# Threshold attention with a dense block: q and k loaded as 32-token by 32-dim quadrant blocks and transposed by VectorE in SBUF instead of by TensorE through PSUM

## Chip, cores and metric

One core of one Trainium2 chip. The metric is the device time of one execution in microseconds (us). Three or four executions of each kernel were timed, and the median is quoted. On a single core no second core can tell a slow execution from a fast one, so an execution more than 1.5% above the fastest of its kernel is called slow and left out of comparisons.

## The reference

Attention over 8 batches of 8 heads, 576 tokens, head dimension 64. In each row only the scores within tau of the row's maximum are kept. A dense block of width 2,048 follows, with h·relu6(h+3)/6 as its activation.

```python
scale  = 1.0 / np.sqrt(64)
scores = scale * np.matmul(q, k.transpose(0, 1, 3, 2))          # 8 x 8 x 576 x 576
thresh = np.max(scores, axis=-1, keepdims=True) - tau           # tau = 0.02
scores = np.where(scores >= thresh, scores, -1e9)
attn   = softmax(scores)                                        # (sum + 1e-9)
x      = np.matmul(attn, v) -> 4608 tokens x 512
h      = x @ w_in                                               # 512 -> 2048
out    = (h * np.clip(h + 3.0, 0.0, 6.0) / 6.0) @ w_out         # 2048 -> 512
```

## The kernel before

The work is cut into 16 "quads" of four heads, each quad into two pairs of heads, and each quad into nine "slots". A slot makes 128 rows of scores for two heads, and in slot 8 the last 64 tokens of all four. In every slot TensorE makes the scores of the next slot, and hidden and output products of an earlier batch. VectorE copies the scores out of PSUM (where this kernel's TensorE results go) into SBUF (where its loads go) and takes their maxima; GpSimd makes the small bias (tau less the maximum); ScalarE masks and takes exponentials; GpSimd normalises into `pn`; and one DMA transpose on SyncE's queue turns `pn` into `pT`, one slot later. TensorE multiplies `pT` by v ("the attention product") in slot 6 for the first pair and in slot 1 of the next quad for the second.

q and k come in natural layout, in pieces (runs of bytes that lie together) of 256 bytes, and have to be transposed to have the head dimension on the partitions:

```python
def main(i, h):                                   # i: q or k
    src = (q, k)[i]
    nc.sync.dma_start(out=nat[quad][i][0][:, :, h, :],
                      in_=src[b, 4 * g + h, 0:512, :].rearrange("(p t) d -> p t d", t=4))
...
def transpose_main(pair, i):
    main = nat[pair // 2][i][0]
    ps = ps_m.tile([P, 512], F32, tag="m", name="tp")
    for t in range(4):
        nc.tensor.transpose(ps[:, t * P:(t + 1) * P], main[:, t, 2 * (pair % 2):2 * (pair % 2) + 2, :], identf[:])
    def evict():
        if i == 0:
            nc.scalar.activation(out=qkT[pair][0][:, 0:512], in_=ps[:], func=Act.Copy, scale=scale)
        else:
            nc.scalar.copy(out=qkT[pair][1][:, 64:576], in_=ps[:])
    return evict
```

The loop over slots, cut to the order in which things are issued:

```python
for n, sl in enumerate(queue):
    if slot == 4 and quad + 2 < NQUAD:
        load_quad(quad + 2)                       # only lists the loads; they start below
    ...                                           # exponentials of the slot before
    sm_max(sl)
    if slot != 6 and todo1:
        ...                                       # hidden product, relu, gate
    ...                                           # output product, masks
    if slot == 1 and quad > 0:   av_main(2 * quad - 1)
    elif slot == 2 and quad > 0: av_rest(quad - 1)
    elif slot == 6:              av_main(2 * quad)
    elif slot > 2 and quad + 1 < NQUAD:
        ...                                       # TensorE transposes q or k (slots 3, 4, 5, 7, 8)
    queue[n + 1].tiles = scores(queue[n + 1].quad, queue[n + 1].slot)
    if prev is not None:
        sm_norm(prev)                             # pn of the slot before, and its DMA transpose
    flush()                                       # stores
    start(loads, 2 if n < 3 else 1)               # one step of two q or k loads, on SyncE's queue
    start(vcasts or casts, 1 if n else 0)         # v and weight loads, on GpSimd's queue
```

The transpose of slot 3, which completes the first pair, is issued at the end of slot 4, and slot 6's attention product needs it.

Of the kernel before, what the change touches and what calls it, by code (L numbers as in the profile page):

```python
# [21 lines left out]
def kernel(  # L22
# [49 lines left out]
    casts = []  # L72
    vcasts = []

    def load_quad(quad):
        b, g = divmod(quad, 2)
        nat[quad] = []
        for nm in "qk":
            nat[quad].append((nat_pool.tile([P, 4, 4, D], F32, tag=nm + "m", name=nm + "m"),
                              nat_pool.tile([64, 4, D], F32, tag=nm + "r", name=nm + "r")))  # L80

        def main(i, h):
            src = (q, k)[i]
            nc.sync.dma_start(out=nat[quad][i][0][:, :, h, :],
                              in_=src[b, 4 * g + h, 0:512, :].rearrange("(p t) d -> p t d", t=4))

        def rest(i):
            src = (q, k)[i]
            nc.sync.dma_start(out=nat[quad][i][1][:],
                              in_=src[b, 4 * g:4 * g + 4, 512:S, :].rearrange("h p d -> p h d"))  # L90

        for n in range(2):
            for i in range(2):
                loads.append(lambda n=n, i=i: [main(i, 2 * n + a) for a in range(2)])
        loads.append(lambda: [rest(i) for i in range(2)])

    def load_v(b):
        vm = v_pool.tile([P, H, 4 * D], BF16, tag="vm", name="vm")
        vr = v_pool.tile([P, NPAIR, D], BF16, tag="vr", name="vr")
        vsb[b] = (vm, vr)  # L100
        for g in range(2):
            vcasts.append(lambda g=g: nc.gpsimd.dma_start(
                out=vm[:, g * 4:g * 4 + 4, :],
                in_=v[b, g * 4:g * 4 + 4, 0:512, :].rearrange("h (p t) d -> p h (t d)", t=4)))
        for a in range(2):
            vcasts.append(lambda a=a: nc.gpsimd.dma_start(
                out=vr[a * 64:(a + 1) * 64, :, :],
                in_=v[b, :, 512:S, :].rearrange("(hp a) p d -> a p hp d", a=2)[a]))
# [4 lines left out]
    def load_weights():  # L113
        for n4 in range(4):
            for ki in range(KI):
                casts.append(lambda n4=n4, ki=ki: nc.gpsimd.dma_start(
                    out=w_in_sb[:, ki, n4 * 512:(n4 + 1) * 512],
                    in_=moe_w_in[ki * P:(ki + 1) * P, n4 * 512:(n4 + 1) * 512]))
        for ni in range(NI):
            casts.append(lambda ni=ni: nc.gpsimd.dma_start(  # L120
                out=w_out_sb[:, ni, :], in_=moe_w_out[ni * P:(ni + 1) * P, :]))
# [5 lines left out]
    load_quad(0)  # L127
    start(loads, 5)
# [3 lines left out]
    identf = singles.tile([P, P], F32)  # L132
    make_identity(nc, identf)
# [9 lines left out]
    def alloc_qk(pair):  # L143
        qkT[pair] = (qk_pool.tile([P, S], F32, tag="qT", name="qT"),
                     qk_pool.tile([P, S + 64], F32, tag="kT", name="kT"))

    def transpose_main(pair, i):
        main = nat[pair // 2][i][0]
        ps = ps_m.tile([P, 512], F32, tag="m", name="tp")
        for t in range(4):  # L150
            nc.tensor.transpose(ps[:, t * P:(t + 1) * P], main[:, t, 2 * (pair % 2):2 * (pair % 2) + 2, :], identf[:])  # L151

        def evict():
            if i == 0:
                nc.scalar.activation(out=qkT[pair][0][:, 0:512], in_=ps[:], func=Act.Copy, scale=scale)
            else:
                nc.scalar.copy(out=qkT[pair][1][:, 64:576], in_=ps[:])
        return evict

    def transpose_rest(pairs):  # L160
        ps = ps_m.tile([P, 512], F32, tag="m", name="tr")
        for n, pair in enumerate(pairs):
            for i in range(2):
                nc.tensor.transpose(ps[:, (2 * n + i) * 64:(2 * n + i + 1) * 64],
                                    nat[pair // 2][i][1][:, 2 * n:2 * n + 2, :], identf[:64, :64])

        def evict():
            for n, pair in enumerate(pairs):
                qT, kT = qkT[pair]
                src = ps[:, 2 * n * 64:(2 * n + 1) * 64], ps[:, (2 * n + 1) * 64:(2 * n + 2) * 64]  # L170
                nc.scalar.activation(out=qT[:, 512:S], in_=src[0], func=Act.Copy, scale=scale)
                nc.scalar.copy(out=kT[0:64, S:S + 64], in_=src[1][0:64, :])
                nc.scalar.copy(out=kT[64:P, 0:64], in_=src[1][64:P, :])
        return evict

    def keys(pair, a, hf):
        kT = qkT[pair][1]
        c0 = 64 * (1 - a) + hf * HALF
        return kT[a * 64:(a + 1) * 64, c0:c0 + HALF]
# [35 lines left out]
    def sm_mask(sl, i):  # L215
        s = sl.s[:, i, :]
        nc.scalar.activation(out=s, in_=s, func=Act.Prelu, bias=sl.bias[:, i:i + 1], alpha=REJECT)  # L217
# [114 lines left out]
    for i in range(2):  # L332
        transpose_main(0, i)()
# [155 lines left out]
```

## Time and profile before

| | before |
|---|---|
| time, median of 3 | 635.71 us (633.47 to 638.48) |
| span of the profiled run, mean granted TensorE clock (share of the full clock) | 631.7 us, 0.965 |
| first slot-8 scores at | 41.6 us |
| quads 1 to 4 (slot 8 to slot 8), while weights come in | 148.3 us |
| quads 5 to 13, mean | 34.34 us |
| quads 14 and 15, for which no q or k is loaded | 33.0, 33.8 us |
| tail after the last quad | 66.1 us |

The five stages are cut at the scores of slot 8, from the trace's records. They add up to the span, so that a difference of two kernels can be put into its stages. The timeline view gives start, length, queue, line, operation and count of what SyncE issues in two slots of one quad, in the kernel before:

```profile
352.78 1.30 SPq L236 DMA_TRANSPOSE pT<-pn  x1
354.17 1.27 SPq L84 DMA_DIRECT2D qm<-in_q_dram  x2
...
356.33 1.29 SPq L236 DMA_TRANSPOSE pT<-pn  x1
```

A transpose takes SyncE 1.3 us to issue and a pair of loads another 1.3. With 3.55 us per slot there is room, and each transpose is issued on time.

### The profile page before, as it was taken

To read this page: it belongs to the slowest core of one execution; us is meant where nothing else is said; L and a number is where in the kernel's file an instruction comes from. 1 tells how busy PE (TensorE), PEld (TensorE's weight loads), DVE (VectorE), ACT (ScalarE), POOL (GpSimd) and SP (SyncE) were. 2 spreads that over 40 slices of the span, in tenths; PEclk is the share of its full clock that TensorE was granted. 3 is DMA by queue.
4 is the path that set the end of the run, shared out by engine and by line. 5 is a ranking of instruction groups with operands and counts; after the bars stand their busy time and mean duration, and the time that the engine had idled before them with its cause. 6 is when DMAs were issued, how large, how long until landed. Compare 5 with 4: busy or idle time off the path is not lost.

```text
span 631.7 us, 11524 instructions
## 1 busy us (share of the span) xinstructions
PE 560.2 (89%) x3840; PEld 323.5 (51%) x3840; DVE 423.8 (67%) x1024; ACT 472.2 (75%) x1062; POOL 305.6 (48%) x646
## 2 busy tenths in 40 slices
PE   4976677876898999899998999899998999898997
PEld 2543334444555555455555555455555555454563
DVE  0453447665787888678887888788886887783260
ACT  2795879647887898779897989788885989773250
POOL 0575568654555654555455544564555545452000
PEclk9987788978999999999999999999998999999999
DMA  4599999999568884787589667788497857453102
GB/s 108 80 188 142 154 147 154 165 137 153 101 102 158 130 175 99 164 119 156 110 158 154 143 137 129 132 141 166 106 170 104 163 116 110 83 102 89 67 4 81
DMA packets 269498, 80.45 MB, mean 127 GB/s; under 512 B 252544, under 2 KB 264832, under 8 KB 269440
## 3 DMA queue, kind: packets, MB, share of 16 engines
q1 hardware_dynamic: 252032, 70.81, 59.1%
q0 software_dynamic: 17408, 8.92, 12.1%
q8 instruction: 30, 0.49, 0.3%
q14 instruction: 28, 0.23, 0.1%
HBM read 36.70 MB, written 9.44 MB: 73 GB/s over the span
## 4 chain that ended last, share of the span: by engine, by line
PE 60%; DVE 11%; DMA 10%; ACT 6%; issue 4%; POOL 2%; DVEq 0%; POOLq 0%
PE s L188 16%; PE o L301 15%; PE h L273 14%; DMA pT<-pn 9%; DVE s L209 7%; PE av L244 6%; ACT s L217 4%; PE tp L151 3%; DVE r L283 2%; PE s L194 2%; POOL pn L229 2%; PE av L248 2%; ACT s L221 1%; DMA pR<-pn 1%; DVE osb L309 1%
## 5 line engine op out<-in xcount | busy, mean ns | idle before, releaser
L229 POOL TENSOR_SCALAR pn<-s,rinv 128x576 bf16<-128x576 f32 x288 | 211.6, 745 | 149.8 <-issue 117.0
L209 DVE TENSOR_SCALAR_CACHE_REDUCE s<-s 128x576 f32<-128x576 f32 x288 | 206.6, 755 | 102.8 <-PE s L188 80.0
L217 ACT ACTIVATE s<-s,bias 128x576 f32<-128x576 f32 x288 | 207.5, 768 | 86.7 <-POOL bias L212 86.5
L221 ACT ACTIVATE s<-s 128x576 f32<-128x576 f32 x288 | 192.7, 671 | 0.4
L188 PE MATMUL s<-kT,qT 64*128 64x288 f32 x1024 | 181.7, 458 | 2.4 <-DVE s L209 2.3
L273 PE MATMUL h<-xT,w_in_sb 128*128 128x288 bf16 x1024 | 146.0, 288 | 2.9 <-DVE g L289 2.0
L301 PE MATMUL o<-w_out_sb,g 128*128 128x512 bf16 x576 | 140.7, 379 | 8.7 <-DVE osb L309 8.7
L273 PEld LDWEIGHTS <-w_in_sb 128*128 128x128 bf16 x1024 | 91.5, 98 | 68.8 <-issue 21.3
L188 PEld LDWEIGHTS s<-kT,qT 64*128 64x128 f32 x1024 | 102.6, 199 | 45.8 <-issue 13.2
L212 POOL TENSOR_SCALAR bias<-m 128x1 f32<-128x1 f32 x288 | 54.7, 190 | 117.0 <-DVE s L209 99.5
L289 DVE SCALAR_TENSOR_TENSOR g<-r,h 128x576 bf16<-128x576 f32 x128 | 96.5, 754 | 17.0 <-ACT r L281 13.7
L301 PEld LDWEIGHTS <-g 128*128 128x128 bf16 x576 | 55.6, 98 | 63.5 <-issue 14.6
L283 DVE TENSOR_SCALAR r<-h 128x576 f32<-128x576 f32 x96 | 72.3, 753 | 0.0
L244 PE MATMUL av<-pT,vm 128*64 128x512 bf16 x256 | 39.0, 429 | 32.8 <-DMA pT<-pn 24.9
L244 PEld LDWEIGHTS <-vm 128*64 128x64 bf16 x512 | 21.3, 116 | 64.3 <-issue 53.5
L221 ACT ACTIVATION_READ_ACCUMULATOR s<-s 128x1 f32 x288 | 54.2, 188 | 0.0
L257 DVE CAST xT<-av 128x512 bf16<-128x512 f32 x32 | 21.9, 685 | 29.8 <-PE av L248 29.8
L281 ACT ACTIVATE r<-h,three 128x576 f32<-128x576 f32 x32 | 23.5, 738 | 23.0 <-PE h L273 23.0
L309 DVE TENSOR_SCALAR osb<-o 128x512 f32<-128x512 f32 x31 | 20.9, 675 | 27.0 <-PE o L301 27.0
L224 DVE RECIPROCAL rinv<-rsum 128x2 f32<-128x2 f32 x144 | 23.0, 160 | 21.2 <-ACT s L221 21.1
L151 PE MATMUL tp<-identf,qm 128*128 128x128 f32 x128 | 21.4, 293 | 5.8 <-DMA qm<-in_q_dram 4.6
L307 ACT ACTIVATE osb<-o 128x512 f32<-128x512 f32 x5 | 3.0, 597 | 31.1 <-PE o L301 31.1
(32 smaller groups left out, 272.3 us busy)
## 6 DMA issues: line engine op xcount, KB each, us to landing
qm<-in_q_dram SPq DMA_DIRECT2D x64, 128.0 KB, 3.0
km<-in_k_dram SPq DMA_DIRECT2D x64, 128.0 KB, 3.2
out_dram<-osb SPq DMA_DIRECT2D x32, 256.0 KB, 2.6
vm<-in_v_dram POOLq DMA_DIRECT2D x16, 256.0 KB, 5.7
pT<-pn SPq DMA_TRANSPOSE x128, 3.5
w_in_sb<-in_moe_w_in_dram POOLq DMA_DIRECT2D x16, 128.0 KB, 4.1
w_out_sb<-in_moe_w_out_dram POOLq DMA_DIRECT2D x16, 128.0 KB, 4.9
qr<-in_q_dram SPq DMA_DIRECT2D x16, 64.0 KB, 2.8
```

The lines of the kernel that those rows point to most:

```text
L151: nc.tensor.transpose(ps[:, t * P:(t + 1) * P], main[:, t, 2 * (pair % 2):2 * (pair % 2) + 2, :], identf[:])
L188: nc.tensor.matmul(tiles[a][:, hf, 0:HALF], qkT[pair][0][a * 64:(a + 1) * 64, t * P:(t + 1) * P], keys(pair, a, hf), start=True, stop=True)
L209: nc.vector.tensor_scalar(out=sl.s[:, i, :].rearrange("p (a b) -> p a b", a=2), in0=ps[:, :, 0:HALF], scalar1=1.0, scalar2=None, op0=Alu.m ...
L212: nc.gpsimd.tensor_scalar(out=sl.bias[:, i:i + 1], in0=sl.m[:, i:i + 1], scalar1=-1.0, scalar2=tau, op0=Alu.mult, op1=Alu.add)
L217: nc.scalar.activation(out=s, in_=s, func=Act.Prelu, bias=sl.bias[:, i:i + 1], alpha=REJECT)
L221: nc.scalar.activation(out=s, in_=s, func=Act.Exp, accum_out=sl.rsum[:, i:i + 1])
L229: nc.gpsimd.tensor_scalar(out=pn[:, i, :], in0=sl.s[:, i, :], scalar1=sl.rinv[:, i:i + 1], scalar2=1.0, op0=Alu.mult, op1=Alu.mult)
L244: nc.tensor.matmul(ps[a * 64:(a + 1) * 64, :], vm[:, 2 * hp + a, c * D:(c + 1) * D], pT[:, 5 * a + c, cols], start=(c == 0), stop=False)
L273: nc.tensor.matmul(hps[:, hf, 0:HALF], w_in_sb[:, ki, ni * P:(ni + 1) * P], xT[b][:, ki, hf * HALF:(hf + 1) * HALF], start=(ki == 0), stop ...
L283: nc.vector.tensor_scalar(out=r[:], in0=hps[:, :, 0:HALF], scalar1=3.0, scalar2=0.0, op0=Alu.add, op1=Alu.max)
L289: nc.vector.scalar_tensor_tensor(out=g.rearrange("p (a b) -> p a b", a=2), in0=r[:], scalar=6.0, in1=hps[:, :, 0:HALF], op0=Alu.min, op1=A ...
L301: nc.tensor.matmul(o_ps[0], gbuf[:, ni, mt * P:(mt + 1) * P], w_out_sb[:, ni, :], start=(ni == 0), stop=(ni == NI - 1))
```

## The change

Intent: take the transposes of q and k off TensorE (2.4 us per quad) and their evictions off ScalarE, and let VectorE transpose 32x32 blocks in SBUF. For that q and k must arrive as blocks of 32 tokens by 32 dims, which halves the piece from 256 to 128 bytes. q moves to GpSimd's queue, k stays on SyncE's. The scale goes into the mask, v gets the token order of the new k in eight loads per batch instead of four, ScalarE takes four relus per quad instead of one, output rows are stored in plain order, and the weight casts start sooner.

```diff
+        def load_q(a, j, n0, n1):
+            h = 4 * a + 2 * g
+            c = 32 * (2 * a + j)
+            nc.gpsimd.dma_start(out=nat[quad][0][c:c + 32, n0:n1, :, :].rearrange("p n k d -> p (n k) d"),
+                                in_=q[b, h + n0:h + n1, :, 32 * j:32 * j + 32].rearrange("n (k r) d -> r (n k) d", r=32))
+
+        def load_k(a, j, n):
+            h = 4 * a + 2 * g + n
+            c = 32 * (2 * a + j)
+            nc.sync.dma_start(out=nat[quad][1][c:c + 32, n, :, :],
+                              in_=k[b, h, :, 32 * j:32 * j + 32].rearrange("(r o) d -> r o d", o=18))
...
-    def transpose_main(pair, i):
...
+    def transpose_q(pair):
...
+        nc.vector.transpose(out=qT[:], in_=nat[pair // 2][0][:, pair % 2, :, :].rearrange("p k d -> p (k d)"))
+
+    def transpose_k(pair):
...
+        nc.vector.transpose(out=kT[:, 0:2, :, :], in_=nk[:, 0:10, :].rearrange("p (i j) d -> p i j d", j=5))
+        nc.vector.transpose(out=kT[:, 2:4, 0:4, :], in_=nk[:, 10:18, :].rearrange("p (i j) d -> p i j d", j=4))
...
         sm_max(sl)
+        if slot in (3, 4, 7, 8) and quad + 1 < NQUAD:
+            pair = 2 * quad + 2 + (slot > 6)
+            if slot in (3, 7):
+                transpose_q(pair)
+            else:
+                transpose_k(pair)
...
-            r = mm1_relu(h, on_act=(slot == 1))
+            r = mm1_relu(h, on_act=(slot in (3, 4, 7, 8)))
...
-        start(loads, 2 if n < 3 else 1)
-        start(vcasts or casts, 1 if n else 0)
-        if n > 18:
+        start(loads, 2 if n < 2 else 1)
+        start(qcasts, 2)
+        start(vcasts, 2)
+        if n > 6:
             start(casts, 1)
```

The loads of a quad are still listed at slot 4: k goes out in slots 4 to 7, one pair per slot; q in slots 4 and 5, two per slot.

## The prediction

> **What bounds the kernel now.** I read the page first (busy shares and the 40 slices), then the table by windows, then the timeline of one steady stretch, because a share over the whole span mixes three stages.
>
> ```profile
> PE 560.2 (89%) x3840; PEld 323.5 (51%) x3840; DVE 423.8 (67%) x1024; ACT 472.2 (75%) x1062; POOL 305.6 (48%) x646
> PE   4976677876898999899998999899998999898997
> DMA  4599999999568884787589667788497857453102
> PE 60%; DVE 11%; DMA 10%; ACT 6%; issue 4%; POOL 2%; DVEq 0%; POOLq 0%
> ```
>
> The chain that ended last is 60% TensorE, but the slices show that TensorE is full only from about the tenth slice on (160 us). Before that the DMA row is full and TensorE is at 6 or 7 tenths. The table by windows (columns: length, then busy us and instruction count of each engine, granted clock, DMA share, GB/s) says the same:
>
> ```profile
> 100.00:140.00 40.00, 29.47 (x198) 17.10 (x196) 25.14 (x62) 26.63 (x64) 25.70 (x53) 0.83 1.05 158
> 300.00:340.00 40.00, 39.74 (x290) 22.93 (x289) 32.53 (x78) 34.65 (x78) 21.29 (x45) 1.00 0.73 137
> ```
>
> So there are three stages: (a) 15 to 160 us, DMA queues full, weights being cast in; (b) 160 to 566 us, TensorE 95 to 99% busy; (c) 566 us to the end, the dense tail, which the change does not touch. One step of stage (b), a slot with a q transpose, from the timeline (start us, busy us, engine, line, operation):
>
> ```profile
> 311.61 0.60 PE L151 MATMUL tp<-identf,qm 128*128 128x128 f32 x4
> 312.14 1.24 PE L188 MATMUL s<-kT,qT 64*128 64x288 f32 x8
> 312.38 0.58 ACT L155 ACTIVATE qT<-tp 128x512 f32<-128x512 f32 x1
> 313.31 1.15 PE L273 MATMUL h<-xT,w_in_sb 128*128 128x288 bf16 x8
> 314.30 1.03 PE L301 MATMUL o<-w_out_sb,g 128*128 128x512 bf16 x4
> 315.17 0.60 PE L151 MATMUL tp<-identf,km 128*128 128x128 f32 x4
> 315.70 1.24 PE L188 MATMUL s<-kT,qT 64*128 64x288 f32 x8
> ```
>
> Start to start, TensorE spends 1.17 us on scores, 0.99 on h, 0.87 on o and 0.53 on the transposes: 3.56 us, which is the distance of the two score groups. There is no hole; TensorE sets this slot, and the change takes out 0.53 us of it. The waits name what stands close behind:
>
> ```profile
> ACT s L217 <- POOL bias L212: 86.5, 97, 6.0
> PE av L244 <- DMA pT<-pn: 24.9, 14, 5.1
> POOL pn L229 <- issue: 117.0, 85, 1.6
> ```
>
> ScalarE's mask waits for the small bias on GpSimd, and TensorE's attention product waits for the DMA transposes of the probabilities. Both matter below.
>
> **What the Trainium skill says.** "VectorE: DVE Perf Modes", section "The three transpose paths", gives VectorE 311 ns for 128x128 bf16, in 32x32 blocks only; no run here has one yet. "DMA: Bandwidth & Descriptors", section "Why small descriptors are slow (HBM only)", states a fixed cost per packet beside the bytes. The trace's packet records agree: on the hardware queue the median packet takes 9 ns at 4 B, 18 at 256 B, 84 at 2,048 B, so about 8.6 ns plus 0.037 ns per byte. On GpSimd's queue, 31 ns for 256 B read, 59 for 1,024, 98 for 2,048: about 21.5 ns plus the same slope. The same page, section "SWDGE vs HWDGE vs iDMA", says that GpSimd computes the descriptors of its own DMAs in software. The trace agrees that the time grows with the pieces: GpSimd's DMA instruction took 576 ns with 128 pieces, 651 with 256, 806 with 512, about 0.5 us plus 0.6 ns per piece. "TensorE: Matmul & The Clock Gate", Part 1, says that an idle array falls to half clock after about 3.4 us; here the attention product after the long wait at 54 us took 1.92 us, against 1.05 at full clock.
>
> **The change part by part.** Stage (b), per group of four heads (a "quad", nine slots; 15 of the 16 quads prepare a following one).
>
> TensorE, removed: 16 transposes of 128x128 in four slots, 4 x 0.53 = 2.1 us, and four small ones in a fifth slot, 0.3 us: 2.4 us per quad. TensorE's own work in a quad, from the starts: scores 9 x 1.17 = 10.5, h 8 x 0.99 = 7.9, o 9 x 0.87 = 7.8, attention products 2 x 1.3 + 0.9 = 3.5, transposes 2.4: 32.1. The quads from 190 to 566 us (by the slot-8 scores) take 32.8 to 37 us, mean 34.2 (376/11). So 2.1 us is waiting, and without the transposes TensorE alone would need 29.7.
>
> ScalarE, removed: evictions of 18.8 + 18.1 + 6.8 + 6.6 + 6.2 = 56.5 us, 3.5 per quad. Added: the relu moves to ScalarE in slots 3, 4, 7 and 8 instead of slot 1, three more per quad at 738 ns = 2.2 us. Its issue period in such a slot: two masks 1.36, two exponentials with their accumulator reads 1.43, relu 0.64: 3.43 us. TensorE would need 3.03 there. So in those four slots ScalarE takes over as the limit, unless it can lag and catch up in slots 5, 6 and 0 to 2, where it needs 2.79. The hidden tile has one PSUM buffer, so the lag allowed is about 0.4 us (o and scores 2.04 us against relu, gate and a hand-over 1.6).
>
> VectorE, removed: three relus per quad, 2.3 us. Added: per pair one transpose of 576 elements and two of 320 and 256. At one element per 0.96 GHz cycle plus the roughly 0.15 us by which its 576-element operations here exceed that (755 ns against 600), an estimate of 0.75 + 0.48 + 0.42 = 1.65 us, 3.3 us per quad. Its work becomes about 29 us per quad: 12.3 row maxima, 6 gates, 3 relus, 3.3 transposes, 4.5 for reciprocals and evictions. Tight, but under TensorE.
>
> If nothing else moved, the quad would fall by between 0.5 us (ScalarE fully in the way) and 2.4 us; I take 2.0, over 13 quads 26 us. At the front, the first score needs eight software DMAs of 576 pieces (0.85 us each) and the k loads, then transposes without TensorE at half clock; I take 3 us off the 14.6 us at which it starts now. In stage (a) the evictions that go are up to 3.5 us per quad on ScalarE, of which I take 1 for 4 quads: 4 us. Sum of gains: 33 us.
>
> Costs. GpSimd: each quad issues four q loads of 32 x 36 = 1,152 pieces, 0.5 + 0.69 = 1.2 us each by the fit, two at the end of slot 4 and two of slot 5, straight before the biases of slots 5 and 6. GpSimd's slot becomes 0.4 + 1.5 + 2.4 = 4.3 us, longer than TensorE's 3.0 to 3.3. Each bias comes up to 2.3 us late; ScalarE has about 0.5 us of slack and VectorE's reciprocal some 2 us, so I put 1 us per quad on the path: 13 us. The v loads double in number (eight per batch instead of four) at about 0.65 us, in other slots: nothing.
>
> DMA: q and k go from 2 x 36,864 packets of 256 B at 18 ns to 2 x 73,728 of 128 B. For k, 8.6 + 4.7 = 13.3 ns; for q on GpSimd's queue, 21.5 + 4.7 = 26 ns (estimates from the fits). Per quad over 16 engines: 5.2 us before, 3.8 + 7.5 = 11.3 after. The DMA share in stage (b), 0.73 of 34.2 us = 25, becomes 31 of 32: nearly full. The product at slot 6 needs the transpose issued at the end of slot 4, and 3.2 us (its landing) already stands in the chain in about half of the quads. A fraction of a microsecond per quad, 0.5 x 13 = 6 us. In stage (a), already full, 4 quads x 1 us = 4 us, since the weight casts are spread more thinly.
>
> Sum: 635.7 - 33 + 13 + 6 + 4 = 626; I lean a little further to the gain, as the q loads may cost GpSimd less than the fit: 624 us.
>
> **The rivals.** One: GpSimd or DMA becomes the bound. For it: 4.3 us slots twice a quad, a DMA share near one, and long landings in stage (a). Against it: GpSimd is 48% busy and can catch up in slots 6 to 8. If both costs are twice what I took, 650 us. Two: ScalarE inherits the limit in the four relu slots and the TensorE saving is hidden anyway; for it 3.43 against 3.56 us before, so only 0.5 us per quad come through; against it, the lag. That would make 640 to 645. Three: the engines do decouple, TensorE's 2.4 us come whole and the waits shrink: 600 to 605.
>
> **Range and chances.** The three gains and losses are each uncertain by about half, which gives some 20 us either way: 602 to 652. The limits of 2% are 623.0 and 648.4. With the centre at the lower limit: faster 0.44, within 2% 0.37, slower 0.19.
>
> **What would show each step.** TensorE busy falls by about 55 us and its score groups in slots 3, 4, 7 and 8 follow each other in 3.1 to 3.4 us instead of 3.56; if 3.45 or more, ScalarE took over. VectorE's transposes show 0.75, 0.48 and 0.42 us; if about twice that, VectorE is the bound and the prediction is wrong. GpSimd's q issues show 1.2 us; the mask's wait for bias grows in slots 5 and 6. The 128 B packets show 13 and 26 ns; the DMA share after 180 us is 0.85 or more; the wait of the attention product for its transpose grows. The tail after the last attention product stays 65 us.

## The result

| | before | changed |
|---|---|---|
| time, median of 4 | 636.52 us | 695.20 us (692.37 to 698.62) |
| span of the profiled run, clock | 631.7 us, 0.965 | 694.5 us, 0.899 |
| first slot-8 scores at | 41.6 us | 45.4 us |
| quads 1 to 4 | 148.3 us | 163.5 us |
| quads 5 to 13, mean | 34.34 us | 39.12 us |
| quads 14 and 15 | 33.0, 33.8 us | 32.9, 34.9 us |
| tail | 66.1 us | 65.7 us |

The changed kernel is slower: the ratio is 1.0929, with a 95% interval of 1.0859 to 1.0999, and its results are correct. A ratio here is the mean time of one kernel's fast runs over the mean of the other's fast runs of the same rounds, so it isn't quite the ratio of the medians. Of the 62.8 us between the two spans, quads 5 to 13 make 9 x 4.78 = 43.0, quads 1 to 4 make 15.2 and the front 3.8. The two quads for which nothing is loaded make 1.0, and the tail gains 0.4. So the loss lies where q and k are loaded.

The page of the changed kernel (busy shares, the TensorE and DMA rows of the slices, the shares of the chain that ended last):

```profile
PE 561.5 (81%) x3472; PEld 307.0 (44%) x3520; DVE 434.5 (63%) x1077; ACT 450.6 (65%) x945; POOL 373.4 (54%) x744
...
PE   2857585867878798796979798797979699898997
...
DMA  7999999979796985979589995979688995546202
...
PE 42%; DMA 16%; DVE 11%; ACT 7%; POOL 6%; issue 5%; DVEq 0%; POOLq 0%
```

TensorE is down from 89% to 81% of the span and from 60% to 42% of the chain, and DMA is up from 10% to 16% of it. TensorE has fewer instructions (3,472 for 3,840: 320 transposes went, and 48 output products are missing from the changed kernel's trace), but the same busy time. Nowhere before the last quads does the TensorE row show the runs of nines that it had. The second of the prediction's two windows:

```profile
300.00:340.00 40.00, 33.81 (x224) 18.32 (x228) 28.31 (x71) 28.10 (x62) 23.20 (x47) 0.91 0.87 124
```

In the steady stretch every engine but GpSimd is less busy, the granted clock is 0.91 instead of 1.00, the DMA share is 0.87 instead of 0.73, and fewer bytes go through (124 GB/s for 137). Nothing is the bound by its busy share, so something waits. The waits (us in all, times, longest us):

```profile
ACT s L206 <- POOL bias L201: 130.8, 99, 12.8
...
PE av L234 <- DMA pT<-pn: 79.7, 21, 6.7
...
DVE qT L159 <- DMA nq<-in_q_dram: 12.1, 3, 7.1
```

The attention product's wait for its DMA transpose grew from 24.9 us to 79.7, by 55 us of the 63. The mask's wait for the bias grew by 44 us, but ScalarE isn't on the chain all that time. The third line is the front of the run, where VectorE waits for the first q. Where the 55 us arise is seen in the timeline of TensorE in one quad, slots 3 to 6:

```profile
346.01 1.24 PE L177 MATMUL s<-kT,qT 64*128 64x288 f32 x8
...
349.13 1.24 PE L177 MATMUL s<-kT,qT 64*128 64x288 f32 x8
...
352.42 1.24 PE L177 MATMUL s<-kT,qT 64*128 64x288 f32 x8
353.59 1.04 PE L291 MATMUL o<-w_out_sb,g 128*128 128x512 bf16 x4
359.44 2.12 PE L234 MATMUL av<-pT,vt 128*64 128x512 bf16 x8 [4.81 <-DMA pT<-pn]
...
362.05 2.29 PE L177 MATMUL s<-kT,qT 64*128 64x288 f32 x8
```

The score groups come 3.12 and 3.29 us after each other. The first is slot 4, which a k transpose had made 3.56; the second is slot 5, which had only the four small ones and took 3.30 before, so it gained nothing. Then TensorE stands for 4.81 us before slot 6's attention product, and afterwards the product takes 2.12 us and the scores 2.29, against 1.05 and 1.24 at full clock: the array fell to half clock in the wait, as the Trainium skill, "TensorE: Matmul & The Clock Gate", Part 1, quoted in the prediction, says. From score group to score group (median of quads 4 to 13), slots 3, 4 and 8 went from 3.56, 3.56 and 3.52 us to 3.12, 3.12 and 3.08, but slot 6 from 3.95 to 9.62 and slot 7 from 3.56 to 4.48; the rest are within 0.05 us of what they were. The loss of a quad stands in slots 6 and 7. Over the whole run the scores' mean rose from 458 to 495 ns and the product's from 429 to 512, which is most of why TensorE is as busy as before with less to do. In the chain of waits of the changed kernel (start, length, what) the same spot reads:

```profile
352.25 7.05 DMA pT<-pn
...
359.44 2.12 PE av L234 x8
```

The transpose of slot 3, issued at 352.25, took 7.05 us to land; in the kernel before, the transpose at this place of the chain took 3.19. SyncE's queue in the same stretch:

```profile
355.96 4.19 SPq L226 DMA_TRANSPOSE pT<-pn  x1
...
361.56 6.08 SPq L226 DMA_TRANSPOSE pT<-pn  x1
```

Beside the slow landing, SyncE itself is held up: the next two transposes take 4.19 and 6.08 us to issue instead of 1.3, so everything behind them in that queue goes late. What was issued just then on GpSimd (timeline, changed kernel):

```profile
352.17 1.67 POOL L86 DMA_DIRECT2D nq<-in_q_dram  x2
...
355.88 1.67 POOL L86 DMA_DIRECT2D nq<-in_q_dram  x2
```

That is coincidence in time, not yet a cause. Taking all of quads 4 to 13 from the trace's records, the median time from issue to landing of the transpose of slots 0 to 8:

```
slot            0    1    2    3    4    5    6    7    8
before        4.3  3.6  3.4  3.2  3.6  3.6  3.3  3.3  4.8  us
changed       4.1  4.3  3.7  7.1 10.8  7.2  3.3  3.2  3.8  us
```

Exactly the three slots that fall on the q loads are slow. (The time counts from the start of issuing; in slots 4 and 5 issuing itself now takes 3.9 and 5.0 us of it, in slot 3 still 1.3.) The new instructions themselves, in the groups of the changed kernel (after the bars: busy us and mean ns of one, then the idle time before them):

```profile
L86 POOL DMA_DIRECT2D nq<-in_q_dram x68 | 56.0, 826 | 0.9 <-POOLq L451 0.9
...
L159 DVE STREAM_TRANSPOSE qT<-nq 128x576 f32<-128x576 f32 x32 | 24.8, 774 | 12.1 <-DMA nq<-in_q_dram 12.1
...
L164 DVE STREAM_TRANSPOSE kT<-nk 128x320 f32<-128x320 f32 x32 | 16.1, 504 | 0.0
```

k's second transpose, of 256 elements, takes 402 ns. The packet records say how q travels. k's 128-byte pieces on SyncE's queue are packets of 128 bytes, 13 ns in the median and 19 in the mean. q's pieces on GpSimd's queue are not: they move in packets of 4,096 bytes, 32 pieces each, 561 ns in the median and 676 ns in the mean, with smaller packets for what is left of each load. A tenth of these packets take 208 ns or less and a tenth 1,253 or more, which suggests that part of their time is itself waiting. The Trainium skill, "DMA: Bandwidth & Descriptors", section "Queues, rings and completion order", says that each DMA engine takes turns between the queues at packet granularity, finishing a whole packet first. Read that way, a DMA transpose stands behind a lump of about 0.6 us each time that an engine turns to q. The records show the packet's size and its time; no view shows whose turn it is.

### The profile page after: what moved, and what is told of

Same layout as the page of the kernel before. It is cut to its first block, busy times and chain, and to the rows that moved or that the text cites. A ratio compares the mean times of both kernels' runs of the same rounds, so it can differ in the third digit from the quotient of the medians.

```text
span 694.5 us, 10893 instructions
## 1 busy us (share of the span) xinstructions
PE 561.5 (81%) x3472; PEld 307.0 (44%) x3520; DVE 434.5 (63%) x1077; ACT 450.6 (65%) x945; POOL 373.4 (54%) x744
## 4 chain that ended last, share of the span: by engine, by line
PE 42%; DMA 16%; DVE 11%; ACT 7%; POOL 6%; issue 5%; DVEq 0%; POOLq 0%
DMA pT<-pn 16%; PE s L177 11%; PE h L263 10%; PE o L291 10%; PE av L234 6%; DVE s L198 5%; POOL pn L219 4%; ACT s L206 3%; ACT s L211 2%; DVE g L279 2%; DVE r L273 2%; PE av L238 2%; ACT r L271 2%; PE s L183 2%; POOL vt L116 1%
## 5 line engine op out<-in xcount | busy, mean ns | idle before, releaser
L177 PE MATMUL s<-kT,qT 64*128 64x288 f32 x1024 | 203.2, 495 | 18.9 <-DVE kT L165 9.5
L263 PE MATMUL h<-xT,w_in_sb 128*128 128x288 bf16 x1024 | 150.6, 294 | 8.0 <-DVE g L279 7.3
L177 PEld LDWEIGHTS s<-kT,qT 64*128 64x128 f32 x1024 | 114.3, 216 | 87.2 <-DVE s L198 41.7
L291 PE MATMUL o<-w_out_sb,g 128*128 128x512 bf16 x528 | 134.4, 379 | 12.1 <-DVE osb L299 9.7
L234 PE MATMUL av<-pT,vt 128*64 128x512 bf16 x256 | 49.7, 512 | 87.7 <-DMA pT<-pn 79.7
L271 ACT ACTIVATE r<-h,three 128x576 f32<-128x576 f32 x75 | 54.8, 732 | 74.5 <-PE h L263 74.2
L234 PEld LDWEIGHTS <-vt 128*64 128x64 bf16 x512 | 25.9, 122 | 118.0 <-issue 98.2
L86 POOL DMA_DIRECT2D nq<-in_q_dram x68 | 56.0, 826 | 0.9 <-POOLq L451 0.9
L273 DVE TENSOR_SCALAR r<-h 128x576 f32<-128x576 f32 x53 | 39.9, 753 | 0.5 <-PE h L263 0.4
L116 POOL DMA_DIRECT2D vt<-in_v_dram x64 | 36.1, 566 | 0.0
```

The lines of the kernel that those rows point to most:

```text
L86: nc.gpsimd.dma_start(out=nat[quad][0][c:c + 32, n0:n1, :, :].rearrange("p n k d -> p (n k) d"), in_=q[b, h + n0:h + n1, :, 32 * j:32 * j ...
L177: nc.tensor.matmul(tiles[a][:, hf, 0:HALF], qkT[pair][0][a * 64:(a + 1) * 64, t * P:(t + 1) * P], keys(pair, a, hf), start=True, stop=True)
L234: nc.tensor.matmul(ps[a * 64:(a + 1) * 64, :], vt[:, 4 * a + hp, a + c, :], pT[:, 5 * a + c, cols], start=(c == 0), stop=False)
L263: nc.tensor.matmul(hps[:, hf, 0:HALF], w_in_sb[:, ki, ni * P:(ni + 1) * P], xT[b][:, ki, hf * HALF:(hf + 1) * HALF], start=(ki == 0), stop ...
L271: nc.scalar.activation(out=r[:], in_=hps[:, :, 0:HALF], func=Act.Relu, bias=three[:])
L291: nc.tensor.matmul(o_ps[0], gbuf[:, ni, mt * P:(mt + 1) * P], w_out_sb[:, ni, :], start=(ni == 0), stop=(ni == NI - 1))
```

## The experiments

First theory: q's loads on GpSimd's queue, in slots 4 and 5 on top of k's, delay the DMA transposes, and slot 6's attention product pays. Rivals: GpSimd's own time for the q loads (the bias comes late); plain DMA throughput, as there are twice as many pieces; the work moved to VectorE and ScalarE. Each edit below is against the changed kernel if nothing else is said, and "before" is the kernel before, run again on the same chip. The cuts leave out the argument `parts` of load_quad, which lists q or k alone, and, in e11 to e14, the move of the hidden product that e7 shows.

### Where q is loaded: slots 1 and 2, or SyncE's queue, long pieces, or nearly not at all

e1: the q loads stay on GpSimd but go out in slots 1 and 2, where no k is loaded.

```diff
+        if slot == 1 and quad + 2 < NQUAD:
+            load_quad(quad + 2, parts="q")
         if slot == 4 and quad + 2 < NQUAD:
-            load_quad(quad + 2)
+            load_quad(quad + 2, parts="k")
```

> The changed kernel with one edit: the four q loads of a quad are issued at the ends of slots 1 and 2 instead of 4 and 5; same loads, same queue, same pieces. Theory (the 4,096 B packets of the q loads on GpSimd's queue share the 16 DMA engines with the transpose of slot 3, whose landing TensorE awaits in slot 6): the wait goes, quads with loads fall from about 39.5 us to 34 to 35, time 630 to 650 us. Rival GpSimd (1.7 us of DMA issue per slot delays bias and normalising): the issue only moves, and lands beside the v loads, time 685 to 705 us. Rival throughput (twice as many small pieces fill the DMA engines on the whole): 685 to 705 us.

Measured: 660.26 us (before 635.92), ratio 1.0405 (1.0328 to 1.0482), correct. The long landings moved with the loads: 6.9, 8.3 and 6.5 us in slots 0 to 2, and 3.7 in slot 3. Quads 5 to 13 take 35.80 us. The time is 10 us above the theory's range and 25 below the rivals'. So the place of q's loads alone is worth 35 us. What is left of the loss beside e6 (below) stands in slots 4 and 5, which take 3.98 and 4.51 us for 3.12 and 3.29 in e6; why there was not taken apart.

e2: the q loads stay in slots 4 and 5 but go through SyncE's queue.

```diff
-            nc.gpsimd.dma_start(out=nat[quad][0][c:c + 32, n0:n1, :, :]...
+            nc.sync.dma_start(out=nat[quad][0][c:c + 32, n0:n1, :, :]...
```

> The changed kernel with the q loads on the SyncE queue, same slots, behind the transpose in the same queue. Theory: the transpose of slot 3 is ahead of q in one queue and lands in about 3.5 us; the wait in slot 6 goes; time 630 to 650 us. Rival GpSimd: its 1.7 us per slot goes too, so it also expects 640 to 660 us. Rival throughput: the pieces cost 13 ns each instead of some 20, so it improves only in part, 670 to 690 us.

Measured: 654.69 us, ratio 1.0303 (1.0233 to 1.0373), correct. Landings in slots 3 to 5: 3.2, 4.3, 4.3 us. Quads 5 to 13 take 35.76 us. The same pieces at the same place, through the other queue, cost 40.5 us less. The time is above the theory's range and in that of rival GpSimd, so e2 doesn't part these two. Slot 6 is down to 4.62 us, as the theory said, but slot 1, with the second pair's product, now takes 6.39 (3.62 in the changed kernel): the wait has moved, which e12 takes up.

e3: the q loads of the changed kernel with the same bytes in rows of 4,608 bytes. The numbers land in the wrong places, so the result is wrong (relative error 1.34); the row maxima change, the work doesn't.

```diff
-                                in_=q[b, h + n0:h + n1, :, 32 * j:32 * j + 32].rearrange("n (k r) d -> r (n k) d", r=32))
+                                in_=q[b, h + n0:h + n1, :, :].rearrange("n s d -> (n s d)").rearrange(
+                                    "(j r f) -> j r f", j=2, r=32)[j])
```

> The changed kernel with the q loads reading contiguous rows of 4,608 B (wrong result on purpose: other elements of q land in the tile), same bytes, queue and slots; 32 pieces instead of 1,152 per load. Theory: what delays the transpose is the time that the q packets hold the engines; it falls to under a half, landing of the slot-3 transpose about 4 to 5 us, time 645 to 665 us. Rival GpSimd: the issue falls from 0.83 to about 0.55 us per load, a third of the loss goes, 670 to 680 us. Rival throughput: all of the extra DMA work goes, 635 to 650 us.

Measured: 651.11 us, ratio 1.0232 (1.0147 to 1.0317). Landings 4.9, 5.2, 3.9 us. A 4,608-byte packet takes 291 ns in the mean, less than half of the 676 ns that 4,096 bytes in 32 pieces take. So the pieces, more than the bytes, make the packets long. The edit also cuts GpSimd's time per load from 0.84 to 0.52 us, so the gain isn't the packets' alone.

e4: q is loaded for the first two quads only and reused by the others (wrong, relative error 1.26).

```diff
...
-        else:
+        elif quad < 2:
             for a, j in aj:
                 qcasts.append(lambda a=a, j=j: load_q(a, j, 0, 2))
```

> The changed kernel without the q loads from quad 2 on: the q tiles of quads 0 and 1 are used again (wrong result on purpose). It bounds what the q loads cost in all. Every theory that blames the q loads expects quads of 33 us as in the last ones, 610 to 635 us. If the engines' new balance (relu on ScalarE, transposes on VectorE) were the cause, it would stay above 670 us.

Measured: 623.26 us, ratio 0.9798 (0.974 to 0.9856). Landings 3.2, 3.4, 3.4 us; quads 5 to 13 take 32.92 us. The q loads cost 695.2 - 623.3 = 72 us. It also sizes the gain: everything else in the change, the costs of k and v included, is worth 635.9 - 623.3 = 12.7 us, not 33. Work on VectorE and ScalarE is all still there, so that rival falls.

### Is the load alone enough?

e5: the kernel before, untouched, with the changed kernel's q loads added into a tile that nobody reads.

```diff
+                extra.append(lambda h=h, c=c, j=j: nc.gpsimd.dma_start(
+                    out=nq[c:c + 32, 0:2, :, :].rearrange("p n k d -> p (n k) d"),
+                    in_=q[b, h:h + 2, :, 32 * j:32 * j + 32].rearrange("n (k r) d -> r (n k) d", r=32)))
...
             load_quad(quad + 2)
+            load_extra(quad + 2)
...
+        start(extra, 2)
```

> The kernel before with the changed kernel's four q loads per quad added (GpSimd's queue, ends of slots 4 and 5, 128 B pieces) into tiles that nothing reads; nothing else changed. Theory: this alone reproduces the wait in slot 6: the landing of the slot-3 transpose goes from 3.2 to about 7 us and each of the 14 quads with loads grows by 3 to 5 us, time 680 to 705 us. If it needed the change's new balance of engines as well, it would stay under 660 us.

Measured: 707.78 us in its one run that counts as fast, 718.79 to 728.75 in the other three (before 635.06). Correct. The profile is of a run that counts as slow (723.94 us), though the fast one is well above the kernel before too. In it, landings in slots 3 to 5 are 7.4, 11.0 and 7.9 us, and quads 5 to 13 take 40.82 us, while the two quads without loads take 33.0 and 35.4. The disturbance is reproduced without any other part of the change. Its size was expected too small, by at least 3 us; q's old loads are still in SyncE's queue here as well, which may be why.

### Both moves together, and the attention product moved

e6 = e1 and e2 together: q on SyncE's queue in slots 1 and 2.

```diff
-            nc.gpsimd.dma_start(out=nat[quad][0][c:c + 32, n0:n1, :, :]...
+            nc.sync.dma_start(out=nat[quad][0][c:c + 32, n0:n1, :, :]...
...
+        if slot == 1 and quad + 2 < NQUAD:
+            load_quad(quad + 2, parts="q")
         if slot == 4 and quad + 2 < NQUAD:
-            load_quad(quad + 2)
+            load_quad(quad + 2, parts="k")
```

> The changed kernel with the q loads on the SyncE queue and at the ends of slots 1 and 2: with the three runs that have one edit or none it makes a square of queue against slot. The slot effect alone took 35 us, the queue effect 41. If the two cures are the same one (the slot-3 transpose set free), this is about as the queue alone, 650 to 655 us; if GpSimd's issue time is a separate cost, it is lower than the slot edit alone by that cost, 635 to 650 us. Throughput alone would leave it at 655.

Measured: 636.40 us (before 635.06), ratio 0.9992 (0.9919 to 1.0064), correct. Landings are as before (3.3, 3.5, 3.5) and yet nothing is gained over the kernel before. An undisturbed transpose still takes about 3.3 us to land, and with slots now shorter the product of slot 6 comes that much sooner.

e7 = e6 with the first pair's attention product one slot later (the hidden product that slot 7 did moves to slot 6).

```diff
-        if slot != 6 and todo1:
+        if slot != 7 and todo1:
...
-        elif slot == 6:
+        elif slot == 7:
             av_main(2 * quad)
```

> The kernel with q on the SyncE queue in slots 1 and 2, and the attention product moved from slot 6 to slot 7 (slot 7 then has no h, slot 6 has one): the slot-3 transpose gets a slot more to land. If the fixed 3.2 us of an undisturbed landing still holds TensorE in slot 6, this saves 0.5 to 1.5 us per quad, 625 to 640 us, and may beat the kernel before. If the remaining loss lies elsewhere (odd quads with the v loads, GpSimd's biases), it changes by under 5 us.

Measured: 597.98 us, ratio 0.9399 (0.9354 to 0.9444), correct; quads 5 to 13 take 31.71 us. That is 27 us below the range expected. In a window of this run:

```profile
300.00:340.00 40.00, 39.09 (x279) 21.49 (x276) 37.12 (x92) 34.72 (x76) 26.50 (x56) 1.00 0.96 158
```

The DMA engines are busy 0.96 of the time, more than the 0.87 of the changed kernel, with every 128-byte piece in place, and TensorE is at 39.09 of 40 us. Plain throughput as the cause falls with that.

e8 = e2 with two GpSimd operations in slots 4 and 5, in place of the time that issuing q took GpSimd. Expected at 0.745 us each, they took 0.675 in the run, 1.32 us per slot where q's two issues had taken 1.69.

```diff
+        if slot in (4, 5) and quad + 2 < NQUAD:
+            for i in range(2):
+                nc.gpsimd.tensor_scalar(out=scratch[:, i, :], in0=source[:], scalar1=1.0, scalar2=1.0,
+                                        op0=Alu.mult, op1=Alu.mult)
```

> The changed kernel with q on the SyncE queue in its own slots (654.7 us), and two needless GpSimd instructions of about 0.745 us at the ends of slots 4 and 5, where the q issue stood: GpSimd's occupancy comes back without its packets. Rival GpSimd: the biases of slots 5 and 6 come 1.5 us late again, 670 to 690 us. Theory: mostly hidden, 655 to 665 us.

Measured: 667.98 us, ratio 1.0518 (1.045 to 1.0586), correct. It lies just above what the first theory gave and just below what the rival gave: GpSimd's time is a cost of its own, 667.98 - 654.69 = 13.3 us, but not the larger one. From e4 up, the 72 us now split, if the parts add up: 654.7 - 623.3 = 31.4 for q on SyncE's queue in k's slots, 13.3 or somewhat more for GpSimd's time, and the rest, 695.2 - 668.0 = 27.2, for what GpSimd's queue does beyond that. (The runs are of different calls, whose runs of the kernel before differ by under 1.5 us.)

### The first theory fails on one point

If slot 6's product is what pays, moving it alone should help the changed kernel too.

e9: the changed kernel with only the move of the product (the diff of e7).

> The changed kernel as it is (q on GpSimd's queue, slots 4 and 5), with the attention product alone moved from slot 6 to slot 7. The transfers are untouched, so the landing of the slot-3 transpose stays near 7 us; only TensorE asks for it one slot (about 3.1 us) later. Theory: most of the 4.8 us wait goes, GpSimd's delay (13 us measured) and the pressure on the queues stay: 640 to 660 us. If the wait were only where another limit shows itself (GpSimd, throughput), it would come back elsewhere: 680 us or more.

Measured: 708.99 us (before 633.75), ratio 1.1169 (1.1094 to 1.1244), correct: worse than the 695.2 of the changed kernel, where the first theory expected a gain. The timeline of TensorE in one quad of e9, slot 7's product and then slot 1's:

```profile
407.35 1.05 PE L234 MATMUL av<-pT,vt 128*64 128x512 bf16 x8
...
423.33 1.92 PE L234 MATMUL av<-pT,vt 128*64 128x512 bf16 x8 [4.99 <-issue]
```

Slot 7's product doesn't wait any more, as the theory said. But slot 1's now does, for 4.99 us. The view names no releaser there ("issue"), but by the records slot 7's transpose landed at 423.24, just before. SyncE's queue in e9, the transposes of slots 4, 5 and 7:

```profile
404.43 3.20 SPq L226 DMA_TRANSPOSE pT<-pn  x1
...
409.03 5.26 SPq L226 DMA_TRANSPOSE pT<-pn  x1
...
419.88 1.35 SPq L226 DMA_TRANSPOSE pT<-pn  x1
```

The transposes of slots 4 and 5 still take 3.20 and 5.26 us to issue, and the ones behind them go late: slot 7's goes out at 419.88, 3.45 us before the product that needs it can start. The wait of TensorE in slot 6 had hidden this, as I read it: while it stood, the queue caught up. Hence the second theory: the row of DMA transposes falls behind as a whole while q is loaded over k, and whichever product comes next pays.

e10: the same move in the kernel before, to know what it is worth alone (one TensorE transpose of q changes places with it).

```diff
-        if slot != 6 and todo1:
+        if slot != 7 and todo1:
...
-        elif slot == 6:
+        elif slot == 7:
             av_main(2 * quad)
...
-                evict = transpose_main(nxt + (slot > 6), {3: 0, 4: 1, 7: 0, 8: 1}[slot])
+                evict = transpose_main(nxt + (slot > 5), {3: 0, 4: 1, 6: 0, 8: 1}[slot])
```

> The kernel before with the same move (the product to slot 7, its transpose of slot 7 to slot 6, no h in slot 7): tells how much of the gain of the last version is the move alone. Undisturbed, the landing of 3.2 us stands in the chain in about half of the quads, TensorE bound otherwise: 622 to 632 us. If the move alone gives all of the gain, about 600 us, and the transposes on VectorE are worth nothing.

Measured: 617.15 us, ratio 0.9761 (0.9697 to 0.9825), correct. The gain is larger than expected. The product's wait for its transpose falls from 24.9 to 12.1 us, so that landing probably cost even the kernel before most of these 2.4%; how much the exchange of the small steps adds is not shown.

### Testing the second theory

e11: e1 with the product in slot 7 (q on GpSimd's queue, slots 1 and 2: q and k apart).

```diff
+        if slot == 1 and quad + 2 < NQUAD:
+            load_quad(quad + 2, parts="q")
         if slot == 4 and quad + 2 < NQUAD:
-            load_quad(quad + 2)
+            load_quad(quad + 2, parts="k")
...
-        elif slot == 6:
+        elif slot == 7:
```

> The changed kernel with q on GpSimd's queue in slots 1 and 2 and the product in slot 7. The move of the product made the changed kernel slower (709 against 695 us), since the transposes that the q packets delay in slots 3 to 5 then push the next ones, and slot 1 waits instead. Second theory: it is the backlog of the whole row of transposes that counts, not the one awaited in slot 6; with q in slots 1 and 2 it has five slots to drain before the product of slot 7, and it costs GpSimd's time and the collision with the v loads: 620 to 645 us. First theory (the wait in slot 6 alone): 600 to 620 us.

Measured: 620.91 us (before 636.1), ratio 0.9752 (0.9729 to 0.9775), correct. At the lower edge of the second theory's range and 0.9 us above the first's, so it doesn't part them. Landings in slots 0 to 2 are still 6.8, 8.2 and 6.4 us, but 3.7 in slot 3.

e12: e2 with the product in slot 7 (q on SyncE's queue, slots 4 and 5: q over k).

```diff
-            nc.gpsimd.dma_start(out=nat[quad][0][c:c + 32, n0:n1, :, :]...
+            nc.sync.dma_start(out=nat[quad][0][c:c + 32, n0:n1, :, :]...
...
-        elif slot == 6:
+        elif slot == 7:
```

> The changed kernel with q on the SyncE queue in its own slots 4 and 5 and the product in slot 7. Second theory: on one queue no backlog forms (landings 3.2 to 4.3 us), so the move of the product helps here as it did with slots 1 and 2 (38 us): 605 to 625 us. If slots 4 and 5 are bad in themselves (transfer work beside the transposes of slots 3 to 5, whatever the queue), the move gains little or loses, 645 us or more.

Measured: 670.96 us, ratio 1.0573 (1.0507 to 1.064), correct. A clear miss: the landings are short (3.2, 4.2, 4.1 us), so q's packets are not in the way, and it is still slow. SyncE's queue in slots 4 to 6 of one quad of e12 shows why:

```profile
381.45 1.75 SPq L226 DMA_TRANSPOSE pT<-pn  x1
383.25 1.26 SPq L92 DMA_DIRECT2D nk<-in_k_dram  x2
384.55 1.25 SPq L86 DMA_DIRECT2D nq<-in_q_dram  x2
385.90 1.73 SPq L226 DMA_TRANSPOSE pT<-pn  x1
```

SyncE issues in order, and one slot's share is now 1.75 + 1.26 + 1.25 and gaps, 4.45 us from transpose to transpose, where TensorE's slot is some 3.1 us. In two such slots the queue falls behind by over 2 us, the k loads of slots 6 and 7 leave it little room to catch up, and slot 1's product pays (TensorE's timeline of e12):

```profile
397.16 1.05 PE L234 MATMUL av<-pT,vt 128*64 128x512 bf16 x8 [3.19 <-DMA pT<-pn]
```

So there are two ways to fall behind: through q on GpSimd's queue (its packets, as argued above), and through SyncE's own issue time. Both showed with q and k in the same slots. The last two runs take that away for both queues.

e13: q on SyncE's queue in slots 4 and 5, k in slots 0 to 3, product in slot 7.

```diff
-            nc.gpsimd.dma_start(out=nat[quad][0][c:c + 32, n0:n1, :, :]...
+            nc.sync.dma_start(out=nat[quad][0][c:c + 32, n0:n1, :, :]...
...
+        if slot == 0 and quad + 2 < NQUAD:
+            load_quad(quad + 2, parts="k")
         if slot == 4 and quad + 2 < NQUAD:
-            load_quad(quad + 2)
+            load_quad(quad + 2, parts="q")
...
-        elif slot == 6:
+        elif slot == 7:
```

> q on SyncE's queue in slots 4 and 5, the product in slot 7, and the k loads moved from slots 4 to 7 to slots 0 to 3. Theory (SyncE's issue falls behind where k, q and a transpose share a slot): SyncE has 1.3 us of q and 1.4 of transpose per slot, nothing falls behind, 598 to 615 us. If q is bad beside the transposes of slots 3 to 5 by itself: 645 us or more.

Measured: 596.09 us (before 637.07), ratio 0.9361 (0.9318 to 0.9404), correct; quads 5 to 13 take 31.43 us. It differs from e12 only in when k is loaded, and that is worth 75 us. It is just below the range expected and, with e7 (597.98 us, within the noise), the fastest that was run. From its waits and its DMA issues (median from issue to landing is the last number):

```profile
PE av L237 <- DMA pT<-pn: 20.1, 7, 5.4
```

```profile
nq<-in_q_dram SPq DMA_DIRECT2D x60, 144.0 KB, 4.0
...
pT<-pn SPq DMA_TRANSPOSE x128, 4.0
```

The product waits for its transpose seven times in the whole run, 20.1 us, and q lands in 4.0 us; in the changed kernel it was 79.7 us, and q took 7.8:

```profile
nq<-in_q_dram POOLq DMA_DIRECT2D x60, 144.0 KB, 7.8
...
pT<-pn SPq DMA_TRANSPOSE x128, 4.4
```

e14: as e13, but q on GpSimd's queue.

```diff
+        if slot == 0 and quad + 2 < NQUAD:
+            load_quad(quad + 2, parts="k")
         if slot == 4 and quad + 2 < NQUAD:
-            load_quad(quad + 2)
+            load_quad(quad + 2, parts="q")
...
-        elif slot == 6:
+        elif slot == 7:
```

> The same with q on GpSimd's queue. Theory A (only k on top of q overfills the queue): as the other plus GpSimd's 13 us, 615 to 635 us. Theory B (the q packets on the second queue keep the transposes from the engines, k or no k): landings of slots 3 to 5 stay at 6 to 11 us and the time stays at 660 to 710 us.

Measured: 632.96 us, ratio 0.9941 (0.9886 to 0.9995), correct. The time is as one theory gave and the landings as the other: they stay at 7.1, 8.9 and 7.1 us in slots 3 to 5. So q's loads on GpSimd's queue delay the landings whether or not k is loaded beside them. The hold-up in issuing depends mostly on k: the transposes of slots 4 and 5 take 1.28 and 1.30 us to issue here (medians of quads 4 to 13), 3.93 and 4.96 in the changed kernel; only slot 6's takes 3.04. And without k behind them in SyncE's queue the row has caught up again by slot 7 (3.2 us), and this version is 76 us faster than e9, which differs only in when k is loaded.

All runs with q and k both loaded, side by side (medians, us):

| q's queue and slots, k's slots | product in slot 6 | product in slot 7 |
|---|---|---|
| GpSimd, 4 and 5; k 4 to 7 | 695 (the changed kernel) | 709 (e9) |
| GpSimd, 1 and 2; k 4 to 7 | 660 (e1) | 621 (e11) |
| SyncE, 4 and 5; k 4 to 7 | 655 (e2) | 671 (e12) |
| SyncE, 1 and 2; k 4 to 7 | 636 (e6) | 598 (e7) |
| GpSimd, 4 and 5; k 0 to 3 | not run | 633 (e14) |
| SyncE, 4 and 5; k 0 to 3 | not run | 596 (e13) |

With q over k the later product makes things worse by 14 to 16 us; with them apart it makes them better by 38 to 39. GpSimd's queue for q costs 37 to 41 us in slots 4 and 5 and 23 to 24 in slots 1 and 2, in every row.

## Why the prediction was wrong

The predicted time was 624 us with a range up to 652; it is 695.

**What held.** TensorE's transposes went, and slots 3, 4 and 8 are 3.12, 3.12 and 3.08 us long (predicted 3.1 to 3.4); slot 7 is so too where slot 6 doesn't wait (3.12 in e4). So ScalarE did not take over. That is the second rival, gone. VectorE's transposes take 774, 504 and 402 ns for 0.75, 0.48 and 0.42 predicted (the working of that estimate rested on a clock rate that no run here shows, and is cut above). k's packets of 128 bytes take 13 ns in the median, as predicted. The first score starts at 9.5 us instead of 14.6, earlier by 5.1 where 3 was predicted. The tail is 65.7 us. GpSimd's time for the q loads costs 13.3 us (e8 less e2) for 13 predicted, but that is luck: an issue takes 0.84 us, not 1.2, and e8 put back less than the whole, so the effect per us was taken too small.

**The step that failed** is the last of the costs: "A fraction of a microsecond per quad, 0.5 x 13 = 6 us" for the attention product's wait, with "4 quads x 1 us = 4 us" for stage (a). The product was named, its transpose was named, and the DMA share was high as forecast (0.87 in the window, "0.85 or more" predicted). What was missing is that the wait would not come from a share. The transposes go out one per slot on SyncE's queue and each has to be on time; the q loads were put straight over the k loads in that row. The one wait grew by 55 us in the run, and q's loads cost 72 us in all (e4), of which some 13 were GpSimd's. The other 59 stand where the prediction had 10. In quads 5 to 13 the changed kernel takes 6.2 us more than e4 (39.12 less 32.92), and 3.5 more in each of quads 1 to 4 (163.5 less 149.6).

Inside that step three things were wrong:

- q's pieces on GpSimd's queue were priced as single packets of 26 ns. They travel 32 at a time, in packets of 676 ns in the mean, which is 21 ns per piece: less time, but in lumps. The landing of three transposes per quad rose from 3.2 to 3.6 us to 7.1 to 10.8 us, in the changed kernel, and again when only these loads were added to the kernel before (e5).
- SyncE's issue time was not counted at all. It is 1.3 us per transpose and 1.3 per pair of loads when nothing is in the way, and 3 to 6 us for a transpose when q's loads on GpSimd's queue and k's loads on its own are (e9, and the changed kernel).
- A wait was counted at its own length. One of 4.8 us also halves the clock after it: 2.12 us for a product of 1.05 and 2.29 for scores of 1.24. So TensorE's busy time, which was to fall by about 55 us, is 561.5 for 560.2.

**The gain** was oversized as well: 33 us predicted, 12.7 measured with q's cost gone (e4). The steady quads gained 1.42 us each instead of 2.0, and the front and quads 1 to 4 nothing (42.1 and 149.6 us in e4, 41.6 and 148.3 before). Slots 3, 4, 7 and 8 are 0.44 us shorter each in e4, but an undisturbed transpose needs 3.2 us to land, so slot 6's product holds TensorE instead: that slot went from 3.95 to 4.62 us. That is shown by e6 and e7, which differ only in where the product (and one hidden product in exchange) stands: 636.4 and 598.0 us. What was seen in about half of the quads before ("3.2 us already stands in the chain") becomes the limit once the rest is faster. The front was lost to the same wait: scores run ahead of the kernel before up to slot 6 of the first quad, where the product stands for its transpose,

```profile
39.55 2.12 PE L234 MATMUL av<-pT,vt 128*64 128x512 bf16 x8 [5.07 <-DMA pT<-pn]
```

and the first slot-8 scores come 3.8 us late. With the product in slot 7 and the same loads (e9) they come at 41.1 us. One reading of the prediction was a little high: TensorE is 93 to 99% busy in its windows between 180 and 540 us, not 95 to 99.

**The rivals.** The first (GpSimd or DMA as the bound, 650 us) had the right parts and less than half of the size. DMA was never the bound as a share: e7 runs at 0.96 and takes 598 us. The third (600 to 605, decoupled engines) is about what e7 and e13 reach, but only with the product moved. With the product in slot 7 in both, the idea of the change is worth 0.9361 over 0.9761, about 4% (e13 against e10, each by its own kernel before).

**What stays open.** Why 32 pieces in one packet of GpSimd's queue take 21 ns each in the mean, where single pieces on SyncE's queue take 14 (e2, e7), and how much of the slow landings is the size of the packet and how much the time it takes. e3 shows that long rows take most of it away, but they change both. Why e9 is 14 us worse than the changed kernel, rather than equal, was not taken apart either. That the queue as a whole falls behind was tested by moving the loads and the product; no run gave the transposes a queue without any loads.

## What to carry to other kernels

Before loads are moved or cut into smaller pieces, look at what else is issued in those same slots, on each queue and on the issuing engine, and follow the most punctual transfer (here one DMA transpose per slot) to the instruction that needs it. A DMA share or an engine's busy share doesn't show that such a row falls behind; the landing times by slot do. And when a wait is moved away from one place, look for the next consumer of the same queue: it pays if the queue has not caught up.

## What the Trainium skill lacked or had wrong

- "DMA: Bandwidth & Descriptors", section "Issuing engines are not separate DMA queues", says that DMAs of all issuing engines run on the same 16 engines and interleave, and that using several only saves issue time, which is usually small. The choice of queue did more here: slot 3's transpose landed in 3.2 us with q on SyncE's queue (e2) and in 7.1 with q on GpSimd's (the changed kernel), and the whole time differed by 37 to 41 us. And issue time was not small: 1.3 us of SyncE per transpose and 0.63 per load, one after the other, bounded e12, and a transpose that meets q's loads on GpSimd's queue took up to 6.08 us to issue.
- The same page, section "SWDGE vs HWDGE vs iDMA", gives the packet as preferably up to 4,096 bytes, and the trace agrees for small pieces (4,096 bytes, 32 pieces of 128); one piece of 4,608 bytes went as one packet (e3). It gives no time for such a packet of small pieces: 561 ns in the median and 676 in the mean here, beside 13 ns for a single 128-byte packet on SyncE's queue, and 178 in the median and 291 in the mean for the 4,608 bytes in one piece on GpSimd's.
- The same page, section "Anatomy of one DMA", calls the making of descriptors small and variable, and gives no figure by the number of pieces. GpSimd spent 0.69 us in the mean on a load of 576 pieces and 0.84 on one of 1,152, and its time for q cost the kernel about 13.3 us (e8 less e2).
- "VectorE: DVE Perf Modes", section "The three transpose paths", has one figure, for bf16. For 128 partitions of fp32 in 32x32 blocks the runs show 774, 504 and 402 ns for 576, 320 and 256 elements per partition.
